# Spacing of weight conversions in a three-layer fp32 kernel: wider during token mixing, closer from the second channel layer's first value product on

## The chip, the cores and the metric

One core of a Trainium2 chip runs the whole program. The metric is device time in microseconds of one execution. "Before" is the kernel as it stood, "after" the kernel with the change.

## What is computed

The reference chains three layers over a batch of 2 with 768 positions and width 512 (weights come in double precision):

```python
# 1. attention: 8 heads of 64, window of 16 around the query, plus block summaries
scores_all = np.concatenate([scores_l_m, scores_s], axis=-1)
a = np.exp(scores_all - np.max(scores_all, axis=-1, keepdims=True))
x = np.matmul(a / (np.sum(a, axis=-1, keepdims=True) + 1e-09), v_all)
# 2. first channel layer, gated
k = np.maximum(xk @ w_k, 0.0)
v = k * k @ w_v
r = 1.0 / (1.0 + np.exp(-(xr @ w_r)))
x = r * v
# 3. token mixing, then the second channel layer
xt = x.transpose(0, 2, 1)
h = np.maximum(xt @ w_tok1, 0.0) @ w_tok2
u = x + h.transpose(0, 2, 1)
h2 = np.maximum(u @ w_ch1, 0.0) @ w_ch2
return (u + h2).astype(np.float32)
```

The change is in layer 3: token mixing is 768 to 256 to 768 per column, the second channel layer 512 to 1536 to 512 per position.

## The kernel before

**Products.** Every fp32 operand is held as a pair hi, lo of reduced-precision halves, and every product is three matmuls: hi by hi, hi by lo, lo by hi (mm3, L541).

**Weight conversions.** The weights arrive as 64-bit words. One call of Weights.step converts one block of 128x512 of them, and this is the unit that the change hands out. It is one instruction on ScalarE (wst, L153), two on VectorE (wf, L157 shift and L163 combine), one on ScalarE (w, L174, the hi half) and one on GpSimd (w, L175, the lo half). For the later chunks of the second channel layer two such blocks make a Fold. Its second conversion also forms sums of the blocks (L185, on VectorE and GpSimd), and the sums get hi and lo halves as well: four more rounded tiles.

**Layer 3.** c_phase is the token mixing of the second batch half, with the transposed input of the first chunk between (plain_prep, utr and u). d_phase is the second channel layer in three chunks of 512 positions. Chunk 0 is computed plainly, in 12 rounds: gate(k) makes a 128x512 block of hidden values in 12 matmuls (go, L541). relu_split turns it into the pair gh on ScalarE (L781) and gl on VectorE (L782). whole(k) adds its value product into four accumulators in 12 matmuls (o, L980). gate(k + 1) stands ahead of whole(k). Here "k0" to "k11" are these rounds. Chunks 1 and 2 use seven products of quarter blocks (part, m at L541, with combinations on VectorE at L843) in place of eight, and need the Folds of w_ch1 and a transposed input with sums of its own (chan_prep: utr L867, f L869, sums L185, u L174 and L175). That input of chunk 1 is made while rounds k9 to k11 of chunk 0 run.

**Who sets the order.** Generators yield the estimated cost of each piece of matmul work. The loop at the end collects these costs as credit, and each time 3 units (S4COST) have come in it calls Weights.step. A product whose weights are not there yet calls Weights.step itself until they are. The queues are then ordered by a scheduler at build time, where relu_split, the sums and the combinations go ahead of other work by priority. Within one conversion ScalarE's L153 and VectorE's L157 keep their program order.

Of the kernel before, what the change touches and what calls it, by code (L numbers as in the profile page):

```python
# [31 lines left out]
SPIN0 = 7  # L32
SPIN, SPIN_UNITS = 1, 8
WFIRST = 2
S2COST, S3COST, S4COST = 4, 2, 3
PT_ACT = ((0, 0), (1, 0), (1, 1))
GB = 4
PIN3, PIN4 = 3, 3
# [19 lines left out]
def fused_kernel(ctx, tc, q, k, v, vt, mu, w_k, w_v, w_r, w_t1, w_t2, w_c1, w_c2, out):  # L58
# [611 lines left out]
    credit = 0.0  # L670
    for n, cost in enumerate(attention()):
# [4 lines left out]
        while credit > 0:  # L676
            got = next(hidden, None)
            if got is None:
                credit = 0.0
# [40 lines left out]
    credit = wcredit = 0.0  # L720
    for got in hidden:
# [4 lines left out]
        if len(wr) == KD:  # L726
            credit += (got or 0.0) * GRATIO
            while credit > 0:
                g = next(gates, None)
                if g is None:  # L730
                    credit = 0.0
# [82 lines left out]
    credit = 0.0  # L814
# [96 lines left out]
    def c_phase():  # L911
# [5 lines left out]
        yield from tok2(1, h1)  # L917
        return uu

    def d_phase(uu):  # L920
        of = out.rearrange("b s e -> (b s) e")
        nck = B * S // CH
        accs = {}
        seq = [0]

        def bring(n):
# [147 lines left out]
    def cd():  # L1074
        uu = yield from c_phase()
        yield from d_phase(uu)

    credit = 0.0
    for got in cd():
        credit += got  # L1080
        while credit > 0:
            credit -= S4COST
            if weights.early:
                weights.step()
    w2.release()
# [54 lines left out]
```

## Time and profile before

| | |
|---|---|
| median of three runs | 505.56 us (503.67 to 506.71) |
| the profiled execution | 506.84 us |
| span in its profile | 504.9 us |
| mean granted TensorE clock | 0.989 of full speed |
| TensorE busy with matmuls | 489.1 us, 97% of the span |
| VectorE, ScalarE, GpSimd busy | 319.6, 239.7, 240.0 us (63%, 47%, 48%) |

The profile is of one execution, and times in it count from the start of its span. The profiled execution's 506.84 us is its span of 504.9 us and 1.94 us around it, and lies 1.28 us above the median of the three runs. Token mixing with S4COST ends, and round k0 of the second channel layer's value products begins, near 310 us. Chunk 0 lasts until about 373 us, chunks 1 and 2 from there to the end.

### The profile page before, as it was taken

The page shows a single profiled execution, that of the slowest core. Times are in us where ns is not written, and L with a number is a line of the kernel's source. Part 1 is how long each engine was busy: PE and PEld are TensorE (multiplying, and loading weights), DVE is VectorE, ACT ScalarE, POOL GpSimd, SP SyncE. Part 2 cuts the span into 40 slices and gives each one's busy share as a digit, 9 for nine tenths or more (in the row PEclk, how much of TensorE's full clock was granted, in tenths as well). Part 3 has the DMA queues.
Part 4 walks back from the last instruction along what each step waited for, and adds up shares of the span by engine and source line. Part 5 has one row for each costly group of instructions (what it writes and reads, how often), then busy time and mean ns, then how long its engine had stood idle before and what let it go on. Part 6 is the DMA issues. An engine that isn't in the chain of part 4 may idle for free.

```text
span 504.9 us, 8793 instructions
## 1 busy us (share of the span) xinstructions
PE 489.1 (97%) x3278; PEld 407.0 (81%) x3278; DVE 319.6 (63%) x638; ACT 239.7 (47%) x541; POOL 240.0 (48%) x294
## 2 busy tenths in 40 slices
PE   7999997999999999999999999999999999999996
PEld 3567785888888898887887787878888999989995
DVE  3888998641514365698789789646479638354352
ACT  1778746872443545655456555554554435011110
POOL 5335587862543457488845535764941813000000
PEclk9899998899999999999999999999999999999999
DMA  8999940321000650000550999629351404163102
GB/s 265 298 294 345 345 124 13 89 80 40 20 1 1 233 186 0 1 0 7 162 167 5 386 398 329 215 91 320 132 167 42 140 30 167 51 201 112 56 1 83
DMA packets 35914, 70.63 MB, mean 140 GB/s; under 512 B 3072, under 2 KB 12288, under 8 KB 35872
## 3 DMA queue, kind: packets, MB, share of 16 engines
q1 hardware_dynamic: 34288, 69.09, 42.1%
q10 hardware_dynamic: 1584, 0.98, 0.7%
q8 instruction: 26, 0.43, 0.4%
q14 instruction: 16, 0.13, 0.1%
HBM read 60.04 MB, written 9.44 MB: 138 GB/s over the span
## 4 chain that ended last, share of the span: by engine, by line
PE 65%; DVE 14%; DMA 11%; ACT 4%; POOL 3%; issue 3%; SPq 1%; DVEq 0%; ACTq 0%; POOLq 0%
PE o L952 12%; PE ko L541 11%; PE m L541 11%; PE acc L541 10%; PE o L980 7%; PE go L541 5%; DMA wst<-in_moe_w_v_dram 4%; PE ro L541 3%; DVE wf L163 3%; DMA wst<-in_moe_w_ch_dram 2%; DMA xT<-in_vt_dram 2%; DVE xk L531 2%; PE pv L425 2%; PE sp L367 2%; DVE xl L533 2%
## 5 line engine op out<-in xcount | busy, mean ns | idle before, releaser
L175 POOL TENSOR_TENSOR w<-wf,w 128x512 fp32r<-128x512 f32 x50 | 69.0, 1387 | 60.8 <-ACT w L174 57.7
L541 PE MATMUL ko<-xh,w 128*128 128x256 f32 x384 | 76.4, 288 | 1.7 <-POOL w L175 0.9
L541 PE MATMUL m<-u,w 128*128 128x256 f32 x504 | 65.1, 283 | 0.7 <-DVE mw L843 0.7
L541 PEld LDWEIGHTS m<-u,w 128*128 128x128 f32 x504 | 63.4, 191 | 2.8 <-DVE mw L843 0.9
L541 PEld LDWEIGHTS ko<-xh,w 128*128 128x128 f32 x384 | 61.2, 188 | 5.4 <-POOL w L175 1.1
L541 PE MATMUL acc<-w,kh 128*128 128x512 f32 x192 | 61.4, 404 | 0.0
L952 PE MATMUL o<-w,gh 128*128 128x512 f32 x192 | 59.1, 391 | 0.0
L541 PE MATMUL ko<-xl,w 128*128 128x256 f32 x192 | 54.4, 283 | 1.1 <-DVE xl L533 1.1
L174 ACT CAST w<-wf 128x512 fp32r<-128x512 f32 x50 | 30.9, 620 | 50.3 <-DVE wf L163 48.5
L163 DVE SCALAR_TENSOR_TENSOR wf<-wst,wf 128x512 int32<-128x512 int32 x50 | 47.5, 958 | 8.8 <-ACT wst L153 7.7
L556 POOL TENSOR_TENSOR kl<-rl,kh 128x512 fp32r<-128x512 f32 x24 | 34.3, 1430 | 36.0 <-ACT kh L555 32.6
L530 POOL TENSOR_SCALAR tmp<-xT,oms 128x256 f32<-128x256 f32 x52 | 38.5, 748 | 21.2 <-DVE xk L531 12.4
L554 DVE TENSOR_TENSOR rl<-rl 128x512 f32<-128x512 f32 x24 | 18.7, 781 | 46.0 <-ACT rl L553 45.8
L387 ACT ACTIVATE pe<-pe,mn 128x120 f32<-128x120 f32 x96 | 36.6, 383 | 14.8 <-DVE mn L385 14.6
L531 DVE SCALAR_TENSOR_TENSOR xk<-xT,mus,tmp 128x256 f32<-128x256 f32 x52 | 39.3, 788 | 5.1 <-POOL tmp L530 4.7
L153 ACT ACTIVATE wst<-wst 128x512 f32<-128x512 f32 x62 | 40.9, 674 | 2.7 <-DMA wst<-in_moe_w_ch_dram 2.7
L541 PEld LDWEIGHTS acc<-w,kh 128*128 128x128 f32 x192 | 35.3, 192 | 7.3 <-ACT pe L387 0.3
L952 PEld LDWEIGHTS o<-w,gh 128*128 128x128 f32 x192 | 34.7, 188 | 6.2
L541 PE MATMUL acc<-w,kl 128*128 128x512 f32 x96 | 37.8, 404 | 0.9 <-POOL kl L556 0.9
L541 PEld LDWEIGHTS ko<-xl,w 128*128 128x128 f32 x192 | 36.2, 188 | 2.2 <-DVE xl L533 1.3
L952 PE MATMUL o<-w,gl 128*128 128x512 f32 x96 | 37.1, 391 | 0.0
L541 PE MATMUL go<-u,w 128*128 128x512 f32 x144 | 35.7, 393 | 0.0
(119 smaller groups left out, 950.9 us busy)
## 6 DMA issues: line engine op xcount, KB each, us to landing
wst<-in_moe_w_ch_dram SPq DMA_DIRECT2D x36, 512.0 KB, 7.3
w<-stored SPq DMA_DIRECT2D x24, 512.0 KB, 5.5
stored<-w SPq DMA_DIRECT2D x24, 256.0 KB, 4.8
wst<-in_moe_w_k_dram SPq DMA_DIRECT2D x8, 512.0 KB, 7.9
wst<-in_moe_w_v_dram SPq DMA_DIRECT2D x8, 512.0 KB, 9.9
wst<-in_moe_w_tok_dram SPq DMA_DIRECT2D x6, 512.0 KB, 4.9
out_dram<-o SPq DMA_DIRECT2D x12, 256.0 KB, 2.3
kw<-in_k_dram SPq DMA_DIRECT2D x9, 320.0 KB, 5.0
```

The source lines that it names most:

```text
L153: a = nc.scalar.activation(top.bitcast(F32), top.bitcast(F32), AF.Prelu, scale=2.0 ** -112, alpha=2.0 ** 32)
L163: nc.vector.scalar_tensor_tensor(wi, top, 3, wi, ALU.logical_shift_left, ALU.bitwise_or)
L174: r = nc.scalar.copy(hi, src)
L175: eng.tensor_tensor(lo, src, hi.bitcast(F32), ALU.subtract)
L387: nc.scalar.activation(pe, pe, AF.Exp, bias=mn[:, p:p + 1], scale=-1.0, accum_out=den[:, p:p + 1])
L530: nc.gpsimd.tensor_scalar(tmp, xT[:, d, x0 - 1:x0 - 1 + MW], om[:, d:d + 1], 1.0, ALU.mult, ALU.mult)
L531: nc.vector.scalar_tensor_tensor(xk[:, d], xT[:, d, x0:x0 + MW], mu[:, d:d + 1], tmp, ALU.mult, ALU.add)
L541: nc.tensor.matmul(o, l, r, start=(first and i == 0), stop=(last and i == 3 * n - 1))
L554: nc.vector.tensor_tensor(rl, rl, rl, ALU.mult)
L556: nc.gpsimd.tensor_tensor(lo, rl, hi.bitcast(F32), ALU.subtract)
L952: nc.tensor.matmul(accs[c][t], l, r, start=(first and j == 0 and i == 0), stop=(last and j == 1 and i == 2))
L980: nc.tensor.matmul(accs[0][t], l, r, start=(k == 0 and i == 0), stop=(k == NF2 - 1 and i == 2))
```

## The change

The spacing of 3 units becomes two: 4 until the first value product of chunk 0 has been begun (accs is then filled, at k0 in whole), and 2.5 from there on. accs moves out of d_phase so that the loop can see it; all lines behind it go up by one (L980 becomes L981, L967 becomes L968).

```diff
-S2COST, S3COST, S4COST = 4, 2, 3
+S2COST, S3COST, S4COST, S5COST = 4, 2, 4, 2.5
...
+    accs = {}
+
     def d_phase(uu):
         of = out.rearrange("b s e -> (b s) e")
         nck = B * S // CH
-        accs = {}
         seq = [0]
...
     for got in cd():
         credit += got
         while credit > 0:
-            credit -= S4COST
+            credit -= S5COST if accs else S4COST
             if weights.early:
                 weights.step()
```

No instruction is added or taken away: the same conversions are made, at other places in the queues. Up to 30.3 units are yielded ahead of the change of spacing (two token-mixing products of 12 x 0.65 and one of the same size for the hidden values, 4 x 0.43 for the transposes, two gates of 4 x 0.65) and some 57 behind it.

**ScalarE's queue ahead of the first value product.** gh is the hidden block of k0, w and wst are conversions, u is the input of chunk 0. Before:

```order
L906 CAST u_3483<-utr_3478 128x512
L906 CAST u_3491<-utr_3486 128x512
L153 ACTIVATE wst_3446<-wst_3446 128x512
L174 CAST w_3452<-wf_3448 128x512
L174 CAST w_3508<-wf_3504 128x512
L153 ACTIVATE wst_3502<-wst_3502 128x512
L174 CAST w_3536<-wf_3532 128x512
L153 ACTIVATE wst_3530<-wst_3530 128x512
L781 ACTIVATE gh_3597<-go_3575 128x512
```

After:

```order
L906 CAST u_3471<-utr_3466 128x512
L906 CAST u_3479<-utr_3474 128x512
L153 ACTIVATE wst_3446<-wst_3446 128x512
L174 CAST w_3509<-wf_3505 128x512
L153 ACTIVATE wst_3503<-wst_3503 128x512
L174 CAST w_3543<-wf_3539 128x512
L781 ACTIVATE gh_3567<-go_3554 128x512
```

Between the last input tile u and gh there were three casts of converted weights and now there are two, and gh stands directly behind the cast instead of behind a further L153.

**ScalarE's queue at the fourth Fold**, between the hidden blocks of k9 (here gh_4002, gh_4008) and k10 (gh_4073). f4_4011 and f4_3995 are the Fold's own blocks, f4_4052 the input of chunk 1, sum_3985 and sum_3976 the last sum of the third Fold, which GpSimd makes. Before:

```order
L781 ACTIVATE gh_4002<-go_3989 128x512
L153 ACTIVATE wst_3966<-wst_3966 128x512
L153 ACTIVATE wst_4009<-wst_4009 128x512
L174 CAST w_3974<-sum_3985 128x256
L869 COPY f4_4052<-utr_4054 128x512
L174 CAST w_4035<-f4_4011 128x512
L174 CAST w_4036<-sum_4040 128x512
L781 ACTIVATE gh_4073<-go_4060 128x512
L174 CAST w_4037<-sum_4044 128x512
```

After:

```order
L781 ACTIVATE gh_4008<-go_3989 128x512
L153 ACTIVATE wst_3993<-wst_3993 128x512
L174 CAST w_3965<-sum_3976 128x256
L153 ACTIVATE wst_3957<-wst_3957 128x512
L869 COPY f4_4052<-utr_4054 128x512
L174 CAST w_4018<-f4_3995 128x512
L781 ACTIVATE gh_4073<-go_4060 128x512
L174 CAST w_4019<-sum_4023 128x512
L174 CAST w_4020<-sum_4027 128x512
```

One L153 of the fourth Fold now stands behind the cast of the third Fold's last sum, and the casts of the fourth Fold's sums stand behind gh of k10.

**VectorE's queue where chunk 0 ends and chunk 1 begins**, as a piece of the difference. L967 (now L968) adds the residual to a finished block of chunk 0, sum and u are the input of chunk 1, m_4186 is a kept product, mw its sum with another:

```order
-L967 TENSOR_TENSOR o<-o,ybuf 128x512
+L968 TENSOR_TENSOR o<-o,ybuf 128x512 x2
 L185 TENSOR_TENSOR sum<-f_4052 128x512
-L967 TENSOR_TENSOR o<-o,ybuf 128x512
 L185 TENSOR_TENSOR sum<-f_4053 128x512
 L175 TENSOR_TENSOR u<-sum,u 128x512
-L967 TENSOR_TENSOR o<-o,ybuf 128x512
+L968 TENSOR_TENSOR o<-o,ybuf 128x512
 L843 TENSOR_TENSOR m<-m,m_4186 128x512
+L968 TENSOR_TENSOR o<-o,ybuf 128x512
 L843 TENSOR_TENSOR mw<-m,m_4186 128x512
-L967 TENSOR_TENSOR o<-o,ybuf 128x512
```

The second residual addition moved ahead of one sum, and the fourth ahead of the first mw.

## Rows read from the trace of the kernel before

**Rows 1.** The page's first part: busy us, share of the span, instructions of each engine

```profile
PE 489.1 (97%) x3278; PEld 407.0 (81%) x3278; DVE 319.6 (63%) x638; ACT 239.7 (47%) x541; POOL 240.0 (48%) x294
```

**Rows 2.** Windows: bounds, length, then each engine's busy us and instructions, clock, DMA

```profile
308.80:310.00 1.20, 0.31 (x1) 0.30 (x2) 0.88 (x2) 0.83 (x2) 1.20 (x1) 1.00 0.95 302
...
310.00:331.00 21.00, 21.00 (x93) 17.06 (x92) 15.78 (x21) 10.91 (x20) 12.93 (x11) 1.00 0.64 204
...
359.00:369.00 10.00, 10.00 (x50) 8.22 (x48) 4.74 (x5) 5.79 (x11) 9.73 (x9) 1.00 0.43 134
...
372.90:380.10 7.20, 6.48 (x53) 6.08 (x51) 6.51 (x12) 3.14 (x7) 1.62 (x1) 1.00 0.46 168
...
380.10:497.50 117.40, 117.40 (x734) 106.12 (x735) 61.68 (x97) 31.43 (x57) 18.72 (x16) 1.00 0.26 85
```

**Rows 3.** Waits of PE and PEld, 285 to 505 us: total us, times, longest

```profile
PE o L980 <- ACT gh L781: 0.9, 1, 0.9
PE m L541 <- DVE mw L843: 0.7, 1, 0.7
...
PEld o L980 <- ACT gh L781: 1.5, 2, 1.2
```

**Rows 4.** Timeline at k0: start, length, instruction, idle before and its releaser

```profile
306.03 1.35 POOL L175 TENSOR_TENSOR w<-wf,w 128x512 fp32r<-128x512 f32 x1 [1.81 <-ACT w L174]
...
306.58 1.35 DVE L163 SCALAR_TENSOR_TENSOR wf<-wst,wf 128x512 int32<-128x512 int32 x1 [0.35 <-ACT wst L153]
...
307.97 0.62 ACT L174 CAST w<-wf 128x512 fp32r<-128x512 f32 x1 [1.41 <-DVE wf L163]
...
309.06 0.57 ACT L781 ACTIVATE gh<-go 128x512 fp32r<-128x512 f32 x1
...
307.73 1.03 PE L867 MATMUL utr<-ident,ybuf 128*128 128x128 f32 x8
```

**Rows 5.** Timeline of ScalarE at the second Fold and k4

```profile
330.80 0.62 ACT L174 CAST w<-sum 128x512 fp32r<-128x512 f32 x1 [0.27 <-DVE sum L185]
331.32 0.59 ACT L781 ACTIVATE gh<-go 128x512 fp32r<-128x512 f32 x1
```

**Rows 6.** Chain of waits: TensorE's rounds from k3's products on: start, length

```profile
326.51 2.75 PE o L980 x12
332.01 3.25 PE o L980 x12
```

**Rows 7.** Timeline from the third and fourth Fold to chunk 1's first products

```profile
357.36 1.19 POOL L185 TENSOR_TENSOR sum<-f 128x256 f32<-128x256 f32 x1
...
363.15 2.53 POOL L175 TENSOR_TENSOR w<-sum,w 128x512 fp32r<-128x512 f32 x2
...
356.35 1.60 DVE L163 SCALAR_TENSOR_TENSOR f<-wst,f 128x512 int32<-128x512 int32 x1
...
358.94 0.69 DVE L163 SCALAR_TENSOR_TENSOR f<-wst,f 128x512 int32<-128x512 int32 x1
...
365.72 2.37 DVE L185 TENSOR_TENSOR sum<-f 128x256 f32<-128x256 f32 x2 [3.01 <-POOL w L175]
...
368.65 0.59 ACT L781 ACTIVATE gh<-go 128x512 fp32r<-128x512 f32 x1
...
370.74 0.58 ACT L869 COPY f<-utr 128x512 f32<-128x512 f32 x1
...
369.51 2.00 PE L980 MATMUL o<-w,gh 128*128 128x512 f32 x8
...
372.86 6.56 PE L541 MATMUL m<-u,w 128*128 128x256 f32 x51
380.09 1.70 PE L541 MATMUL m<-u,w 128*128 128x256 f32 x12 [0.67 <-DVE mw L843]
```

**Rows 8.** Timeline of VectorE and GpSimd: input tiles beside a GpSimd subtraction

```profile
302.11 1.28 DVE L907 TENSOR_TENSOR u<-utr,u 128x512 fp32r<-128x512 f32 x2
...
302.93 1.29 POOL L175 TENSOR_TENSOR w<-wf,w 128x512 fp32r<-128x512 f32 x1 [2.22 <-ACT w L174]
```

## The prediction

> **What bounds the kernel.** I read the busy times first: TensorE has matmuls in 97% of the span [rows 1]. That is too coarse to judge a change which adds no instruction, so the question is where TensorE stands still in the stretch the change can reach, from token mixing (285 us on) to the end. The windows answer it: TensorE is full from 310 to 331 and from 380.1 to 497.5 [rows 2], and it is idle for 1.20 - 0.31 = 0.89 us ahead of the first value product and for 7.20 - 6.48 = 0.72 us ahead of 380.1 [rows 2]. The waits by engine name the two: 0.9 us for gh of k0, and 0.7 us for a combination mw of chunk 1 [rows 3]. A third is seen only in the chain of waits, where a value product of 12 matmuls takes 2.75 us as a rule, but 3.25 at k4, that is 0.50 more [rows 6]; the weight loads' wait for gh (two in all, 1.5 us) belongs to this one and the first [rows 3]. So the change can win back at most 0.9 + 0.5 + 0.7 = 2.1 us, if it makes nothing late. The granted clock is 1.00 in all five windows, idle ones included [rows 2]: these gaps cost their length and nothing through the clock.
>
> Below, all sums are against the profiled execution (506.84 us); the median of the runs is 505.56, so 1.28 is taken off at the end. What can be told from no change in this kernel is about 0.5%, 2.5 us: all the gaps together would not reach it.
>
> **Fewer conversions ahead of k0.** 30.3 units are yielded there: 30.3 / 3 = 10.1 conversions before, 30.3 / 4 = 7.6 now. At k0 gh, itself 0.57 us, waits in ScalarE's queue for a cast at 307.97, which waited 1.41 us for VectorE's combine at 306.58; that combine took 1.35 beside a GpSimd subtraction that began at 306.03 [rows 4]. In the new order one cast fewer stands between the input and gh, and gh is directly behind the last. One combine and one cast less are 1.35 + 0.62 = 1.97 us [rows 4], so gh would end at 309.63 - 1.97 = 307.7; its own matmuls are over by 307.73, when the transposes begin [rows 4], so it cannot end after 307.73 + 0.57 = 308.3 for that reason. TensorE needs it at 307.73 + 1.03 = 308.8. The wait goes: **-0.9 us**.
>
> **The second Fold moves one round later.** Its casts occupy ScalarE until gh of k4 starts at 331.32 [rows 5], which is the 0.50 of k4 [rows 6]. By the new queue it comes a round later, when gh is not late: **-0.5 us**. A price may come instead at the next round, where a combine now stands ahead of gl: at most the stretch of one combine, 1.35 - 0.69 = 0.66 [rows 4, 7], at least nothing; I take nothing, since a round is 5.5 us long (326.51 to 332.01 in the chain [rows 6]) and gl is needed only after the first products with gh.
>
> TensorE thus comes to k11 about 1.4 us earlier: at 369.51 - 1.4 = 368.1 [rows 7].
>
> **The Folds for chunk 1 are what is late next.** At the start 10.1 - 7.6 = 2.5 conversions are missing. A round yields 8 x 0.65 = 5.2 units, so the closer spacing makes up 5.2 / 2.5 - 5.2 / 3 = 0.35 of one each round: seven rounds until it is level, about k7 or k8. By count the fourth Fold, at k9 to k10, is on time. By queue it is not. In the new order one of its two L153 stands on ScalarE behind the cast of the third Fold's last sum, which GpSimd makes at 357.36 and ends at 358.55 [rows 7]. From there it is a cast, an L153, a shift and a combine: bounded below by 0.4 + 0.6 + 0.4 + 0.69 = 2.1 us, so 360.7, and with the third Fold about 0.4 late itself some 361.1; before, the last combine ended at 358.94 + 0.69 = 359.63 [rows 7]. The Fold closes about 1.4 us later (bounds: 0.3, if the third Fold comes 0.8 earlier with TensorE; 3.3, if both combines take the 1.60 of the one at 356.35 in place of 0.69 [rows 7]).
>
> GpSimd is the engine that feels this. From 359 to 369 it is busy 9.73 of 10 us, against 4.74 on VectorE and 5.79 on ScalarE [rows 2], and VectorE's sums for the input of chunk 1 wait 3.01 us for its subtraction pair of 2.53 [rows 7]. Some 0.5 of the 1.4 is absorbed by the gap between GpSimd's earlier pieces, so the sums at 365.72 go to 366.6. Their 2.37 us, a cast of 0.62 and then gh of k11 (368.65 before [rows 7]) follow, so gh is about 0.6 to 0.8 later and the products of k11 start at 370.1 to 370.3 in place of 369.51. TensorE, ready at 368.1, waits here some 2.1 us: **the 1.4 us are given back and 0.6 to 0.8 on top.**
>
> **What the gap at 380 does.** From 369.51 to 379.42 (372.86 + 6.56) TensorE worked almost without a stop, then waited 0.67 for mw [rows 7]. Starting 0.6 to 0.8 later it comes to that point at 380.0 to 380.2. VectorE's side starts from the copy f4 at 370.74 [rows 7]; a sum of the input is now ahead of gl there, which is worth 0.4, so the copy falls between 370.3 and 371.0 and its chain ends between -0.4 and +0.3 of where it did. The residual addition now ahead of the first mw costs 0.6 on VectorE, about one operation of that kind at 128x512 [rows 8], but TensorE has four value matmuls, 4 x 0.23 = 0.9, between, by the 2.75 for twelve of the chain [rows 6]. Resumption is therefore at 380.1 to 380.8 against 380.09. Behind it nothing changes: TensorE is full for 117.4 us [rows 2] with the same matmuls, and the remaining conversions are called for in both kernels at the same places.
>
> **Sum:** -0.9 - 0.5 + 2.1 - 0.5 (most of the 0.67 at 380) is +0.2; by the bounds 0 to +0.7. I take +0.2, the end that TensorE's own work gives. 506.84 + 0.2 = 507.0 as a profiled time, 505.8 against the median.
>
> **Weighing a rule.** The combine, with both inputs in SBUF, takes 0.69 by itself and 1.35 when it begins during a GpSimd subtraction; 307.93 - 0.69 = 307.24 is just about where that subtraction ended, 307.38 [rows 4, 7]. Two operations with one input in PSUM, at 302.11, took 1.28 together, 0.64 each, with a subtraction under way from 302.93 [rows 8]. The Trainium skill (SBUF — State Buffer, Who interferes with whom) states that two-input VectorE work and GpSimd reads exclude each other for a whole instruction; the trace agrees. By that rule closer spacing is bad in itself: it puts more combines behind subtractions. On the rows' own figures it would be 0.66 for each combine caught, and it counts only where VectorE is waited for, at the fourth Fold; that is rival B.
>
> **The rivals.**
> A, *the gains stay.* GpSimd's full stretch from 359 begins as much earlier as TensorE does, because the third Fold's sums and the transposes come 1.4 us earlier too. Then k11 starts at 368.1 and the chain to 380 moves with it: -1.4, and with the last gap closed -2.1. For it: VectorE and ScalarE are half idle there [rows 2]. Against: GpSimd has 0.27 us to spare in 10, and the new order ties the Fold to it. 503.5 to 504.2 against the median; chance 0.25.
> B, *the fourth Fold is caught twice* (slower). Both of its combines begin during subtractions: 2 x (1.60 - 0.69) = 1.8 us [rows 7], paid one for one, since at k11 and at 380 everything already waits. It decides as soon as the Fold closes after 361.1. That gives +0.2 + 1.8 = +2.0, 507.6; with the shifts caught as well, 0.5 each, +3.0, 508.6. For: the closer spacing packs both engines. Against: in the old trace only the first of the two was caught. Chance 0.15.
> C, *the change does next to nothing*: products would call for their weights themselves and even out the spacing. The moved rows speak against it; 505.6, chance 0.05.
>
> **How the numbers follow.** The forecast has 0.55, with its own range 505.0 to 506.6 (bounds 0 to +0.7, and the runs' scatter). Faster by over 0.5% would be below 503.0: A ends at 503.5, so only part of A together with scatter, 0.11. Slower by over 0.5% is above 508.1: the upper part of B and a stray of the forecast, 0.09. The rest, 0.80, is no measurable difference. The range takes in A down to 503.4 and B to 507.7, leaving out 2 in 10.
>
> **What would show it.** Right: no wait for gh at k0; 2.75 in the chain at k4; a new wait of about 2 us at k11's products, for gh; little or no wait near 380; the Fold's last combine ending near 361. Wrong: no wait at k11 (A); two combines of 1.3 us or more near 357 to 362 and a wait of 3 us or more at k11 or near 380 (B); or waits for converted weights in k1 to k8, which I hold excluded.

## The result: 0.7% slower

The changed kernel took 508.39 us in the median of 13 runs (505.1 to 512.28) against 504.38 for 13 runs of the kernel before (503.52 to 506.71); the ratio is 1.0071, with a 95% interval of 1.0051 to 1.0091. Forecast was no measurable change, 505.8 us in a range up to 507.7. The profiled execution took 511.99 us, with a span of 509.9.

Spans are no good measure of so small a change here: TensorE reached the transposes that precede the first value product at 307.73 us before and at 309.10 after, and between 304.5 and 312.7 in the runs below, though everything but the last stretch ahead of them is the same work. I therefore take the **segment** from the start of these transposes (utr x8, at k0) to the end of TensorE's last matmul, both from the timeline: 500.87 - 307.73 = 193.1 us before, 505.85 - 309.10 = 196.8 after. The difference of 3.6 us is 0.7% of the whole, the measured ratio. The profiled executions of a_vadd and wide_spin4 below were in a slower state, with a longer stretch at a lower clock early on, so no segment is read from them, and the ratios leave such runs out.

**The profile after.** The page's first part, as [rows 1]:

```profile
PE 491.6 (96%) x3278; PEld 408.5 (80%) x3278; DVE 321.1 (63%) x638; ACT 239.5 (47%) x541; POOL 240.5 (47%) x294
```

The busy time gives a first hint: the same 3278 matmuls are 2.5 us *more* busy, which already says that some ran slowly. The waits of TensorE from 285 us on, as [rows 3]:

```profile
PE m L541 <- POOL u L175: 1.9, 1, 1.9
PE o L953 <- ACT gh L781: 1.4, 1, 1.4
PE m L541 <- ACT u L174: 0.4, 1, 0.4
```

The wait for gh at k0 is gone. In its place stand a wait for the input of chunk 1 (u, made by GpSimd and ScalarE) and one for gh of chunk 1. TensorE's timeline, first at k0 and then from the end of k10, as [rows 4, 7]:

```profile
309.10 1.03 PE L867 MATMUL utr<-ident,ybuf 128*128 128x128 f32 x8
309.89 2.10 PE L981 MATMUL o<-w,gh 128*128 128x512 f32 x8
...
368.25 0.60 PE L867 MATMUL utr<-ident,ybuf 128*128 128x128 f32 x4
368.61 0.36 PE L541 MATMUL m<-u,w 128*128 128x256 f32 x1
370.87 0.51 PE L541 MATMUL m<-u,w 128*128 128x256 f32 x2 [1.90 <-POOL u L175]
371.81 0.38 PE L541 MATMUL m<-u,w 128*128 128x256 f32 x1 [0.43 <-ACT u L174]
372.30 3.07 PE L981 MATMUL o<-w,gh 128*128 128x512 f32 x8
375.17 0.42 PE L541 MATMUL m<-u,w 128*128 128x256 f32 x1
...
376.87 6.75 PE L541 MATMUL m<-u,w 128*128 128x256 f32 x55
385.06 1.20 PE L953 MATMUL o<-w,gh 128*128 128x512 f32 x4 [1.44 <-ACT gh L781]
```

The eight value products of k11 take 3.07 us, where eight took 2.00 before [rows 7]. The windows of TensorE in that stretch (bounds, length, busy us and count, granted clock, DMA share, GB/s) say why:

```profile
370.00:371.00 1.00, 0.13 (x1) 1.00 1.02 410
371.00:372.00 1.00, 0.57 (x3) 1.00 0.06 21
372.00:373.00 1.00, 0.89 (x4) 1.00 0.00 0
373.00:374.00 1.00, 1.00 (x5) 0.59 0.00 0
374.00:375.00 1.00, 1.00 (x4) 0.50 0.00 0
375.00:376.00 1.00, 1.00 (x4) 0.50 0.00 0
376.00:377.00 1.00, 1.00 (x6) 0.71 0.00 0
377.00:378.00 1.00, 1.00 (x11) 1.00 0.00 0
```

From 369.0 to 372 TensorE hardly worked. Then, while it was busy without a gap, the granted clock stood at its lower level, 1.2 of 2.4 GHz. Added up over one-microsecond windows, 2 x (1 - granted), that is 3.4 us at the lower level, and so up to 1.7 us of TensorE's time; by the table below the same matmuls took 1.41 longer. Before, the clock was 1.00 through this stretch:

```profile
369.00:378.00 9.00, 8.96 (x64) 1.00 0.50 176
```

Both profiles have further stretches at the lower level ahead of 92 us, some 10.2 us in each, so all that follows counts from the transposes at k0 on.

**Where the 3.6 us came from**, point by point as distances from the transposes at k0:

| | before | after | gained or lost |
|---|---|---|---|
| first value product, k0 | 1.96 | 0.79 | -1.17 |
| transposes after k10 | 60.87 | 59.15 | -0.55 more |
| first value product, k11 | 61.78 | 63.20 | +3.14 |
| end of the long run of m | 71.69 | 74.52 | +1.41 |
| TensorE goes on | 72.36 | 75.96 | +0.77 |
| end of the last matmul | 193.14 | 196.75 | 0.0 |

The table tells where TensorE lost time. What set the moment at which it went on is told by the chain of waits of the changed kernel, and that chain passes the slow matmuls by:

```profile
371.83 1.47 POOL u L175
374.93 1.54 DVE u L175 x3
376.47 0.95 DVE o L968 x2
377.42 5.57 DMA out_dram<-o
385.06 1.20 PE o L953 x4
```

It goes from the late input of chunk 1 (u) through two residual additions and the transfer of their output to the first value product of chunk 1. So in this execution a full clock would only have brought TensorE to the wait at 385 earlier. This is argued from the chain; no run takes away the fall of the clock alone.

### The profile page after: what moved, and what is told of

Its sections match the earlier page's. It is cut to its first block, busy times and chain, and to the rows that moved or that the text cites. A ratio compares the mean times of both kernels' runs of the same rounds, so it can differ in the third digit from the quotient of the medians.

```text
span 509.9 us, 8789 instructions
## 1 busy us (share of the span) xinstructions
PE 491.6 (96%) x3278; PEld 408.5 (80%) x3278; DVE 321.1 (63%) x638; ACT 239.5 (47%) x541; POOL 240.5 (47%) x294
## 4 chain that ended last, share of the span: by engine, by line
PE 60%; DVE 17%; POOL 9%; issue 6%; ACT 4%; DMA 4%; SPq 0%; DVEq 0%; POOLq 0%; ACTq 0%
PE o L953 12%; PE m L541 10%; PE ko L541 10%; PE acc L541 9%; POOL w L175 4%; PE sp L367 3%; DVE wf L163 3%; PE pv L425 3%; PE ho L541 2%; DVE xk L531 2%; PE pt L405 2%; PE ro L541 2%; DVE wf L157 2%; PE spin L620 2%; DMA out_dram<-o 1%
## 5 line engine op out<-in xcount | busy, mean ns | idle before, releaser
L541 PE MATMUL acc<-w,kh 128*128 128x512 f32 x192 | 60.2, 397 | 0.0
L174 ACT CAST w<-wf 128x512 fp32r<-128x512 f32 x50 | 30.9, 620 | 51.6 <-DVE wf L163 49.7
L163 DVE SCALAR_TENSOR_TENSOR wf<-wst,wf 128x512 int32<-128x512 int32 x50 | 45.1, 911 | 9.2 <-ACT wst L153 8.1
L153 ACT ACTIVATE wst<-wst 128x512 f32<-128x512 f32 x62 | 40.9, 672 | 2.7 <-DMA wst<-in_moe_w_ch_dram 2.7
```

Of the source, the lines that this page charges most:

```text
L153: a = nc.scalar.activation(top.bitcast(F32), top.bitcast(F32), AF.Prelu, scale=2.0 ** -112, alpha=2.0 ** 32)
L163: nc.vector.scalar_tensor_tensor(wi, top, 3, wi, ALU.logical_shift_left, ALU.bitwise_or)
L174: r = nc.scalar.copy(hi, src)
L541: nc.tensor.matmul(o, l, r, start=(first and i == 0), stop=(last and i == 3 * n - 1))
```

## The experiments

Twelve runs, in three groups. "Waits" are TensorE's marked waits from k0 on to the end of that stretch; "fourth Fold" is the end of VectorE's last combine for chunk 1's first weights, from the transposes at k0; "lower clock" is counted as above.

| run | ratio (95%) | segment | waits | lower clock | fourth Fold |
|---|---|---|---|---|---|
| before | 1 | 193.1 | 1.59 | 0 | 51.9 |
| after | 1.0071 (1.0051 to 1.0091) | 196.8 | 3.77 | 3.4 | 53.9 |
| wide_only | 1.0048 (1.0028 to 1.0067) | 195.5 | 2.37 | 3.4 | 55.2 |
| close_only | 1.0023 (1.0006 to 1.0039) | 194.2 | 2.16 | 0 | 53.6 |
| a_inplace | 1.0027 (1.0006 to 1.0048) | 196.2 | 2.38 | 6.8 | 54.0 |
| a_wfsplit | 0.9983 (0.9964 to 1.0001) | 192.9 | 1.50 | 0 | 53.3 |
| a_spin4 | 1.0005 (0.9985 to 1.0025) | 194.1 | 0 | 0 | 53.9 |
| a_vadd | 1.0018 (0.9992 to 1.0045) | | 2.40 | 0 | 52.4 |
| b_vadd | 1.0008 (0.9990 to 1.0027) | 193.5 | 2.39 | 0 | 51.6 |
| b_wfsplit | 0.9984 (0.9961 to 1.0008) | 192.6 | 1.38 | 0 | 51.8 |
| b_spin4 | 1.0037 (1.0014 to 1.0061) | 195.3 | 0.88 | 0 | 51.9 |
| wide_spin4 | 1.0090 (1.0064 to 1.0117) | | | | 55.2 |
| wf_35 | 0.9947 (0.9917 to 0.9977) | 191.9 | 0.74 | 0 | 52.3 |
| wf_s2 | 1.0015 (0.9982 to 1.0047) | 196.5 | 2.66 | 6.8 | 54.3 |

Segments are of one execution each. They differ from that of before by what the ratios say within the interval's width in all but two, a_inplace and wf_s2, where the profiled execution had 6.8 us at the lower clock.

### Each half of the change alone

```diff
# wide_only
-S2COST, S3COST, S4COST, S5COST = 4, 2, 4, 2.5
+S2COST, S3COST, S4COST, S5COST = 4, 2, 4, 3
# close_only
+S2COST, S3COST, S4COST, S5COST = 4, 2, 3, 2.5
```

Expected of the first:

> Spacing 4 until the first value product, 3 from there on. Theory (the Folds for chunk 1 close late, TensorE waits for chunk 1's input at k11, and its clock falls on the way): nothing makes up the missing conversions here, so the Folds close later still; a wait of 3 us or more around k11, ratio to before 1.006 to 1.015. Rival (the closer spacing is what costs, because it packs conversions onto VectorE and GpSimd): without it the loss is gone, 0.998 to 1.002.

Expected of the second:

> Spacing 3 as before until the first value product, 2.5 from there on. Theory: no conversion is missing at k0, the third and fourth Fold close no later than before, no wait over 1 us at k11 and no fall of the clock; 0.997 to 1.002, with the 0.9 us wait at k0 still there. Rival (closer spacing costs, or the L153 of the fourth Fold behind the cast of the third Fold's last sum is enough by itself): waits at k11 of 1.5 us or more and 1.004 to 1.008.

Measured: 0.48% and 0.23% slower, and their sum is the change's 0.71%. Neither theory has it all. TensorE's waits with the wide spacing alone:

```profile
PE utr L867 <- ACT f L869: 2.0, 2, 1.3
PE o L981 <- ACT gh L781: 0.3, 1, 0.3
```

The Folds close latest of all (55.2), and TensorE waits even for the transposes' copies, 0.75 and 1.29 us, then 0.33. The clock follows, and in this run the slow value products of k11 (2.98 and 1.53 us) stand on the chain of waits. Windows of TensorE:

```profile
366.00:367.00 1.00, 0.00 (x0) 1.00 0.10 33
367.00:368.00 1.00, 0.66 (x4) 1.00 0.96 344
...
369.00:370.00 1.00, 1.00 (x4) 0.53 0.00 0
370.00:371.00 1.00, 1.00 (x4) 0.50 0.00 0
371.00:372.00 1.00, 1.00 (x5) 0.50 0.00 0
```

With the close spacing alone the clock stays at 1.00, there is no wait for u, and yet the fourth Fold closes 1.7 us later than before. So closer spacing does make that Fold late, against my theory; TensorE's waits were only 0.6 us longer than before:

```profile
PE o L981 <- ACT gh L781: 1.0, 1, 1.0
PE o L953 <- ACT gh L781: 0.7, 1, 0.7
PE o L981 <- DVE gl L782: 0.4, 1, 0.4
```

### Is it the clock or the wait?

Four idle matmuls are put on TensorE ahead of chunk 1's first products, in the changed kernel, in the kernel before as a control, and in wide_only.

```diff
         for _ in prep:
             pass
+        spin(4)
         weights.early = False
```

> The changed kernel with four idle matmuls (identity by identity, about 0.5 us each) on TensorE ahead of chunk 1's first products, where it waited 2.3 us and its granted clock then stood at half for 3.2 us. Theory (the fall of the clock is a cost of its own, about half of 3.2 us): no stretch below 0.9 after k10, 1.5 us won back and up to 0.5 lost to the idle matmuls; ratio to before 1.003 to 1.006. Rival (the wait is all of the loss, the slow stretch would have been waited out at 385 anyway): 1.006 to 1.009.

> The kernel before with the same four idle matmuls, a control: there was no fall of the clock there and no wait over 0.7 us, so by the theory of the clock they cost between nothing and their 2 us; ratio to before 1.000 to 1.004. Rival (the idle matmuls, or the other order of TensorE's queue that they bring, are a gain of their own): 0.993 to 0.997, about what they won in the changed kernel.

> Spacing 4 and 3 with the four idle matmuls; without them the ratio was 1.0048 and the clock stood at half for 3.4 us after two waits of 0.75 and 1.29 us. Theory of the clock: no stretch at half, the waits filled; 1.000 to 1.003. Rival (with the wide spacing the late Folds themselves are the loss): 1.004 to 1.007.

In the changed kernel three of the four fell into the wait (they count as two records each):

```profile
364.93 1.02 PE L620 MATMUL spin<-ident 128*128 128x512 f32 x2
365.78 0.60 PE L867 MATMUL utr<-ident,ybuf 128*128 128x128 f32 x4
366.22 2.74 PE L620 MATMUL spin<-ident 128*128 128x512 f32 x6
368.52 0.56 PE L541 MATMUL m<-u,w 128*128 128x256 f32 x1
```

```profile
366.00:368.00 2.00, 2.00 (x9) 1.00 0.72 262
368.00:370.00 2.00, 2.00 (x8) 1.00 0.00 0
370.00:372.00 2.00, 2.00 (x14) 1.00 0.00 0
```

The fourth Fold closes at 53.9 as in the changed kernel, GpSimd's first input tile begins at 60.3 in both, and the value products of k11 begin at 63.2 in both. Yet the clock stays at 1.00, the segment is 2.6 us shorter, and the ratio is 1.0005, even better than I expected. In the kernel before the same matmuls cost 0.37%. So what is late up to k11 doesn't by itself make the difference of 0.66%, and the idle matmuls with the order that they bring are no gain of their own.

But two things went together here: the fall of the clock, and the 1.44 us wait at 385. TensorE's queue is in another order behind the idle matmuls (84 products m ahead of chunk 1's first value product in place of 60), and VectorE waited only 0.79 us for an output transfer. The rival's argument, that the slow stretch would have been waited out at 385 anyway, is thus not excluded by this run, and by the chain of waits above it holds for the profiled execution of the changed kernel. One sign for the clock is in the timed executions of the changed kernel: the only one with a mean granted clock of 0.999 took 505.1 us, the other twelve, at 0.986 to 0.996, took 506.81 to 512.28. It is a single execution, and its waits are not on record.

The third run missed: 1.0090. In that kernel all four idle matmuls (3.59 us in its timeline) landed *ahead* of the transposes that chunk 1's input is made from, and the value products of k11 began at 64.4 in place of 63.0. In its profiled execution an output transfer of 6.02 us stood on the chain of waits again, TensorE waited 2.90 us for gh of chunk 1 behind it, and the clock fell there. Which of these makes the difference to 1.0048, no run separates.

### What makes the fourth Fold late

First, whether it is the shared pair of buffers. VectorE's longest wait for GpSimd in the changed kernel, which the kernel before does not have:

```profile
341.34 0.94 DVE L157 TENSOR_SCALAR wf<-wst 128x512 int32<-128x512 int32 x1 [4.57 <-POOL w L175]
```

a_wfsplit gives conversions a pair of their own. The space for it comes from writing the residual in place, which a_inplace does alone:

```diff
# a_inplace, a_wfsplit
-            o = w2.tile([128, DM], F32, tag="o", bufs=OB, name="o")
-            nc.vector.tensor_tensor(o, accs[c][t], ys[c * NQ + t], ALU.add)
+            o = ys[c * NQ + t]
+            nc.vector.tensor_tensor(o, accs[c][t], o, ALU.add)
# a_wfsplit, with late = [w2] from layer 3 on
-            wf = use.part() if fold else stage.tile([128, 512], F32, tag="wf", ...)
+            wf = use.part() if fold else (late or [stage])[0].tile([128, 512], F32, tag="wf", ...)
```

> The changed kernel with the residual sums written into the input's own tile in place of two output buffers, so that no sum waits for an output transfer. Theory: only the 2.3 us wait of VectorE for the output transfer goes, of which TensorE felt at most its 1.4 us wait at 385; the wait and the clock at k11 stay; 1.004 to 1.007. Rival (the output transfer is the cause): 1.000 to 1.002.

> As the run with in-place residuals, and besides conversions and Fold sums no longer share one pair of buffers in layer 3, so that VectorE's shift of a conversion doesn't wait for GpSimd's subtraction of a Fold sum (4.6 us in the changed kernel). Theory with that wait as its root: the third Fold closes about 2 us earlier, the wait at k11 is under 1 us and the clock stays at its upper level; 0.998 to 1.002. Rival (the place of the fourth Fold's L153 in ScalarE's queue is the root): little changes, 1.004 to 1.007.

> The kernel before with in-place residuals and conversions and Fold sums in buffers of their own. Theory: it has no wait for a conversion buffer in this stretch, so nothing is to be won there, and its output transfers weren't waited for; 0.998 to 1.002. Rival (the split is a gain of its own, not the cure of the change): 0.993 to 0.997.

a_wfsplit came out as expected by the number (0.9983; a_inplace, which lacks only the buffers of its own, has 1.0027, and the intervals don't meet), but only partly for my reason. The 4.57 us wait is gone, and the third Fold closes at 44.4 in place of 44.9, 0.5 earlier and not 2. The other half is that TensorE lost 1.15 us at k6, where gh now stood behind a cast, and came to k11 later (60.9 in place of 59.2). So it waited only 0.35 there and kept its clock:

```profile
PE o L984 <- ACT gh L783: 1.2, 1, 1.2
PE m L543 <- ACT u L176: 0.4, 1, 0.4
```

On the kernel before the same edit gives 0.9984. With it the change is worth nothing, in either direction.

a_inplace removes VectorE's wait for an output transfer (2.25 us at 383.08, see below) and with it TensorE's wait at 385, but the waits for u are the same 1.9 and 0.4, and in its profiled execution the clock stayed down for 6.8 us. With the transfer gone the slow products stand on its chain of waits:

```profile
367.96 3.70 PE o L981 x8
371.87 1.71 PE o L981 x4
```

TensorE comes to chunk 1's first value product 75.97 us from the transposes at k0, as in the changed kernel (75.96), but without a wait just before it, and with 64 products m done in place of 60. The ratio of 1.0027 (seven executions) is better than the 1.004 I gave it and worse than the rival's 1.002, and its interval ends below that of the changed kernel (1.0048 against 1.0051). So the output transfer carries a part of the loss, by the middle values 0.44% of 0.71%. The theory had at most 1.4 us, 0.28%, which the interval still reaches.

Second, the place in the queue. In the changed kernel ScalarE's and VectorE's timelines around the fourth Fold are:

```profile
361.26 0.41 ACT L174 CAST w<-sum 128x256 fp32r<-128x256 f32 x1 [3.55 <-POOL sum L185]
361.57 0.66 ACT L153 ACTIVATE wst<-wst 128x512 f32<-128x512 f32 x1
```

```profile
359.05 1.59 DVE L163 SCALAR_TENSOR_TENSOR f<-wst,f 128x512 int32<-128x512 int32 x1
362.27 0.76 DVE L163 SCALAR_TENSOR_TENSOR f<-wst,f 128x512 int32<-128x512 int32 x1 [1.63 <-ACT wst L153]
```

The cast waits 3.55 us for a sum by GpSimd; the L153 behind it waits as well, with its input long loaded (no load was issued between 347.2 and 365.0), and VectorE's combine waits for that. a_vadd and b_vadd let VectorE make this sum:

```diff
-            sums(piece(m["both"], d), nc.gpsimd, (0, f[:, 0], f[:, 3], ALU.add), adder=nc.gpsimd)
+            sums(piece(m["both"], d), nc.gpsimd, (0, f[:, 0], f[:, 3], ALU.add))
```

> The changed kernel with the third of a Fold's sums made by VectorE in place of GpSimd; all else as changed, the 4.6 us wait for a conversion buffer too. Theory with the fourth Fold's place in the queues as the root (its L153 stands behind the cast of a sum that GpSimd makes late, and GpSimd is full from there): that cast comes earlier, the fourth Fold closes 1 to 2 us earlier, TensorE's wait at k11 is under 1 us and the clock stays; 0.998 to 1.002. Rival (the buffer wait is the root): 1.004 to 1.007.

> The kernel before with that same sum on VectorE. Theory: GpSimd's full stretch ahead of chunk 1 sets the wait of 0.67 us before chunk 1's products already in the kernel before, so relief wins 0.3 to 1.5 us; 0.996 to 1.000. Rival (relief matters only where the Fold is late): 0.999 to 1.002.

The fourth Fold closes at 52.4, 1.5 us earlier, TensorE's two waits at k11 are 0.48 and 0.71, and the clock stays. The ratio is 1.0018, within the theory's range, though its interval reaches 1.0045. On the kernel before, whose fourth Fold is not late, the same edit does nothing (1.0008), as the rival had it: the relief of GpSimd is no gain of its own.

### A kernel that beats both

```diff
# both with the edits of a_wfsplit
# wf_35
+S2COST, S3COST, S4COST, S5COST = 4, 2, 3.5, 2.5
# wf_s2
+S2COST, S3COST, S4COST, S5COST = 4, 2, 4, 2
```

> Spacing 3.5 until the first value product and 2.5 from there on, residuals in place, conversions and Fold sums in buffers of their own. Theory: one conversion less missing than at 4, no wait for a conversion buffer, no wait of 2 us at k11 and so no fall of the clock; 0.995 to 0.999. Rival (lateness of the Folds is set by the closer spacing): 1.002 to 1.005.

> Spacing 4 and then 2, residuals in place and buffers apart. Theory: what is missing at k0 is made up twice as fast, the first Folds close a round earlier, no fall of the clock; 0.995 to 1.000. Rival (closer spacing costs in itself): 1.002 to 1.006, with more waits for gh in k3 to k8.

wf_35 is 0.5% faster than the kernel before (0.9947, 0.9917 to 0.9977). How much of that is the spacing's is not shown: the kernel before with the same buffers has 0.9984 (0.9961 to 1.0008), and the intervals overlap. It keeps what the change was good for: no wait at k0 and none at k4. The fourth Fold closes at 52.3, and the waits are the smallest of all but a_spin4's:

```profile
PE m L543 <- ACT u L176: 0.4, 1, 0.4
PE m L543 <- POOL u L177: 0.3, 1, 0.3
```

wf_s2 missed its forecast. Its Folds come later again (54.3), it waits 2.23 and 0.43 us for u, and the clock falls. So still closer spacing does not make up the lateness, it adds to it: in a_wfsplit, which differs in this spacing alone (2.5 in place of 2), the third and the fourth Fold close 0.9 us earlier (44.4 and 53.3 against 45.3 and 54.3). Why, with buffers apart, no run settles.

## Why the prediction was wrong, by its own steps

**The gains were right.** At k0 -0.9 was forecast, and the first value product came 1.17 earlier; at k4 -0.5, and -0.55 more had come by k10. TensorE reached k11 1.7 us earlier (1.4 forecast).

**"The Folds for chunk 1 are what is late next"** named the right path, but was too small. The value products of k11 start at 372.30, where gh of k11 ends on ScalarE, behind the cast of an input sum; the waits for u lie within that time:

```profile
371.13 0.62 ACT L174 CAST u<-sum 128x512 fp32r<-128x512 f32 x1 [0.79 <-DVE sum L185]
371.66 0.59 ACT L781 ACTIVATE gh<-go 128x512 fp32r<-128x512 f32 x1
```

The close was put at +1.4 us and measured at +2.0: the third Fold, which I had "about 0.4 late", closed 1.1 later (44.9 against 43.8). About half of that is the 4.57 us wait for a conversion buffer, which I had bounded as a stretch of one combine at the next round and set to nothing. That wait was visible in the order, since VectorE's shift stands ahead of gl there. VectorE's sums, put 0.9 later, came 1.7 later, and the start of k11, put 0.6 to 0.8 later, came 1.42 later. TensorE thus lost 3.14 there in place of 2.1.

**"What the gap at 380 does" is the step that failed.** I had TensorE go on at 380.1 to 380.8 against 380.09, with the wait of 0.67 shrunk to almost nothing, worth -0.5. Counted from the transposes at k0 it went on 3.60 later than before, behind a wait of 1.44. I had costed the moved residual addition as one operation of VectorE. Two additions now stood together at 376.39, and the third found both output buffers in flight:

```profile
383.08 0.69 DVE L968 TENSOR_TENSOR o<-o,ybuf 128x512 f32<-128x512 f32 x1 [2.25 <-DMA out_dram<-o]
383.69 0.69 DVE L843 TENSOR_TENSOR m<-m,m 128x512 f32<-128x512 f32 x1
```

Queued behind it was the combination that gh of chunk 1 waits for. The input tile u ahead of it, at 379.56, was 0.96 later than before, the combination 3.55. The DMA of the moved step was left out of my count, and so this wait of 2.25 us stood at nothing without a reason. The chain of waits gives that transfer 5.57 us from 377.42; the same four transfers took 2.6 in the median in the kernel before, and why they took longer is not shown. a_inplace, without this wait, came to 1.0027.

**A second sentence failed ahead of the sum:** "these gaps cost their length and nothing through the clock". It was true of the old gaps, none longer than 0.9 us. I then forecast a new wait of "some 2.1 us" at k11, measured at 1.90 + 0.43, and booked it by length. It was the first wait of that size in the stretch, and the clock went to its lower level behind it: +1.41 on TensorE's next run of work, by the row of 3.07 us and the windows. The Trainium skill (TensorE: Matmul & The Clock Gate, HAM oscillation — how this bites in real kernels) states that a wait between bursts of matmuls can let the clock be throttled, so that the next burst starts cold and runs at half rate. The windows agree on the half rate, 0.50 from 374 to 376 behind that wait, but the burst began at 1.00. In the changed kernel's profiled execution this cost lies beside the transfer and, by the chain, was waited out at 385; in a_inplace and wide_only, where TensorE does not wait there, the slow products are on the chain. a_spin4 against its control b_spin4 shows that the two together, with the order that it brings, are the difference between +0.7% and nothing; how they divide stays open.

As TensorE's timeline has it, the sum was off by 3.4 us: 1.0 more at k11, 1.4 in the slower run, 1.3 more at the gap at 380, less 0.3 gained more at k0 and k4. By the chain, the 1.4 and the 1.3 are one delay, the transfer's.

**Rival B** was the nearest: slower, because the fourth Fold closes late, deciding "as soon as the Fold closes after 361.1". In these terms it closed at 363.03 - 1.37 = 361.7, 1.37 being the later start of the run. Its mechanism did not hold, though: only one of the two combines was stretched (1.59 at 359.05, 0.76 at 362.27), where two were expected; the lateness came through ScalarE's queue, and the rest by the transfer and the clock. That its +2.0 to +3.0 came near the measured +3.6 is luck. **Rival C** is excluded, since the wait at k0 is gone and the change costs 0.71%. **A** failed as argued: GpSimd was busy 9.17 of the 10 us from 362 to 372.

## What to carry to other kernels

When a change moves waits about, price each new wait for what TensorE does after it too: short waits here cost their length, and the clock fell behind crowded ones. Then ask by the chain of waits whether that cost is on the path or beside another. A block of work that is handed out earlier or later in program order still goes through in-order queues: look for the instruction behind which its first step stands, and for the engine that one waits for. And where a step with a transfer moves, count its buffers, for the next step of its kind waits until one is free.

## What the runs showed of the hardware that I had not expected

The granted clock fell not during the wait but behind it, with TensorE fully busy: 0.89 busy and 1.00 granted at 372 to 373, then 0.59 and 0.50. How long it stayed down differed between executions of kernels that waited alike, 3.4 us in the changed kernel and 6.8 in a_inplace (1.9 and 0.4 us of waiting in both). Single waits of 1.15 us (a_wfsplit at k6) and 1.44 us (at 385 in the changed kernel) were followed by no fall in their windows.
